# Hash attention with a mixture of adapters: signs made in place, adapter work regrouped, a tail with sums on TensorE

## The chip, the cores and the metric

The kernel runs on one core of a Trainium2 chip. The metric is device time in microseconds, from the first to the last instruction of the core. Three runs of the kernel before gave 201.65 us in the median (201.6 to 202.56). The engines are named as in the profile: PE is TensorE (matmul), PEld its weight loads, DVE is VectorE, ACT is ScalarE, POOL is GpSimd, SP is SyncE, which here only issues transfers.

## What is computed

Attention for 4 batches of 8 heads, 768 positions, 64 features. Each query and key is hashed to six sign bits by a projection, and a query attends only to keys with the same six bits. The result, seen as 3072 rows of 512 features, goes through a layer with eight low-rank adapters of which each row uses two.

```python
q_bits = (np.einsum('bhsd,dk->bhsk', q, proj) > 0)          # 6 bits
k_bits = (np.einsum('bhsd,dk->bhsk', k, proj) > 0)
mask = q_bucket[:, :, :, None] == k_bucket[:, :, None, :]
scores = np.where(mask, scale * q @ k.T, -1e9)
attn = softmax(scores)                                       # per query
x = (attn @ v).transpose(0, 2, 1, 3).reshape(3072, 512)
# adapters: E = 8, rank r = 16, the best two by gate
logits = x @ w_gate                                          # 3072 x 8
w = softmax over the two largest logits
out = x + sum over the two of  w * ((x @ A[e]) @ B[e])
```

## The kernel before

The work is cut into 16 **pairs** of heads (four per batch). One pair has nine **scores** steps, s = 0 to 8: TensorE fills a PSUM tile of 128 x 1024, ScalarE takes its exponential. Between the scores the program places the other work of the neighbouring pairs: transposes of q and k two pairs ahead, their hash one pair ahead, the weighted sum of the values, the norm. The hash becomes part of the score matmul: `aug` holds 64 rows of q or k, six sign rows (64 to 69) of plus or minus one half, and a constant row, so that scores of unequal buckets come out so low that their exponential vanishes.

```python
def score(self, p, s):
    ps = self.ps_s.tile([P, 1024], F32, tag="s")            # two buffers
    for h, kt, q, n, o in self.pieces(p, s):
        nc.tensor.matmul(out=ps[:, o:o + n], lhsT=aug[0:71, 2*h+1, kt*P:(kt+1)*P], rhs=q, ...)
    nc.scalar.activation(out=self.P_[p][:, s*1024:(s+1)*1024], in_=ps, func=ACT.Exp, scale=128.0)

def pair(self, p, s):                                        # after score(p, s)
    if s == 0: self.norm(p - 1, 0); self.trans(p + 1, 2)
    if s == 1: self.pvmm(p - 1, 1, 0, 2); self.cast(p + 1, 0); self.cast(p + 1, 1)
    if s == 2: self.hash(p + 1)
    if s == 3: self.uniform(p); self.pvmm(p - 1, 1, 2, 5)
    if s == 4: self.pvmm(p - 1, 1, 5, 6); self.norm(p - 1, 1); self.trans(p + 2, 0)
    if s == 5: self.vcast(p + 1); self.trans(p + 2, 1)
    if s == 6: self.pvmm(p, 0, 0, 2); self.xturn(p - 1); self.load(p + 3)
    if s == 7: self.pvmm(p, 0, 2, 4)
    if s == 8: self.pvmm(p, 0, 4, 6)
```

`trans` makes four fp32 transposes on TensorE into one of two `ps_t` buffers and a scaled copy (qkT) on VectorE; `cast` is a GpSimd copy of qkT to bf16 into aug; `hash` makes the signs of four heads and halves in four column tiles, one VectorE compare, and four small DMAs to move the signs to their rows. `pvmm` uses one `ps_v` buffer; `norm` reads it on VectorE and then lets GpSimd copy x to bf16 (xb), which a transposing DMA (`xturn`) turns into xT.

The adapters of batch b run during the pairs of batch b + 1, in groups of **slots** (a slot is 128 of the batch's 768 rows):

```python
def moe_slot(self, p, s):                                    # after pair(p, s)
    b, g = divmod(p - self.PPB - 1, self.PPB)                # PPB = 4 pairs a batch
    groups = ((0, 1), (2, 3), (4,), (5,)) if b < self.B - 2 else ((0, 1, 2), (3, 4, 5))
    ...
    if s == 1: self.lgz(b, slots); self.route_a(b, slots)
    if s == 2: self.route_b(b, slots)
    if s == 3: self.zmtrans(b, slots)
    if 0 <= s - 5 < len(slots): self.delta(b, slots, s - 5)

# lgz (PE):      lz = xT @ [w_gate | A]           one ps_m buffer, PSUM
# route_a (DVE): top = max8(lz gates); d = lz - top1; m = (lz >= top2); (ACT) e = exp(d)
# route_b (DVE): gw = m * e; zm = lz * gw; ss = sum(gw); rt = 1 / ss
# zmtrans (PE):  ztp = zm transposed; zmT = copy of ztp
# delta (PE):    dl = zmT @ Bcat;  (DVE) acc = dl * rt + x;  (SP) DMA of acc to the output
```

lz, ztp and dl share the one buffer of `ps_m`. Batch 3 has no pair after it. Its adapters run within the last pair and in the **tail** after the last exponential, in three groups of two slots; `third(u, part)` makes the weighted sum of the last pair for one third of the slots, `third_x` its normalised rows:

```python
def last_pair(self, p, b):                                   # t = the three groups
    ...
    if s == 3: self.xtrans(p - 1); self.third(0, 0)
    if s == 4: self.third(0, 1)
    if s == 5: self.xtrans(p, t[0]); self.third_x(0, x); self.lgz(b, t[0])
    if s == 6: self.route_a(b, t[0]); self.third(1, 0); self.route_b(b, t[0])
    if s == 7: self.third(1, 1); self.zmtrans(b, t[0], last=True)
    if s == 8: self.xtrans(p, t[1]); self.delta(b, t[0], 0, last=True); self.lgz(b, t[1]); ...
    # after the nine scores
    self.route_a(b, t[1]); self.third(2, 0); self.delta(b, t[0], 1, last=True)
    self.route_b(b, t[1]); self.zmtrans(b, t[1], last=True)
    self.third(2, 1)
    self.delta(b, t[1], 0, last=True)
    self.xtrans(p, t[2], on_act=True); self.lgz(b, t[2]); self.delta(b, t[1], 1, last=True)
    self.route_a(b, t[2]); ...; self.route_b(b, t[2]); self.zmtrans(b, t[2], last=True)
    for i in range(2): self.delta(b, t[2], i, last=True)
```

The **head** is the time before the first exponential. It loads the first pair head by head and makes the first head's signs:

```python
self.warm(19)                                                # small matmuls that keep TensorE busy
self.turn0(0)                                                # transposes and qkT copies, head 0
for e in range(2): nc.vector.tensor_copy(out=self.proj2[...], in_=self.pst[...])
self.half0(0, 0, nc.scalar.copy); self.warm(5)
self.hash0(0, (nc.gpsimd, nc.scalar))                        # hsf (PE), sgnf (DVE), two sign DMAs
self.half0(0, 1, nc.vector.tensor_copy)
self.turn0(1); self.half0(1, 0, nc.gpsimd.tensor_copy); self.half0(1, 1, nc.gpsimd.tensor_copy)
...
self.warm(12)
```

In pair 0 the second head's hash follows score 0 and the loads of pair 2 follow score 3; `load_moe` (the adapters' weights, six transfers issued by GpSimd) follows score 4.

Of the kernel before, what the change touches and what calls it, by code (L numbers as in the profile page):

```python
# [12 lines left out]
F32 = mybir.dt.float32  # L13
# [6 lines left out]
class Emitter:  # L20
# [45 lines left out]
    def prologue(self):  # L66
# [26 lines left out]
        self.warm(19)  # L93
        self.turn0(0)
        for e in range(2):
            nc.vector.tensor_copy(out=self.proj2[64 * e:64 * e + 64, e:12:2],
                                  in_=self.pst[64 * e:64 * e + 64, :])
        self.half0(0, 0, nc.scalar.copy)
        self.warm(5)
        self.hash0(0, (nc.gpsimd, nc.scalar))  # L100
        self.half0(0, 1, nc.vector.tensor_copy)
        self.turn0(1)
        self.half0(1, 0, nc.gpsimd.tensor_copy)
# [12 lines left out]
        self.Bcat = sg.tile([self.ER, self.Dm], BF16, name="Bcat")  # L116
        self.warm(12)


    def turn0(self, h):  # L120
        nc, P = self.nc, self.P
        for i in range(2):
            ps = self.ps_s.tile([P, 384], F32, tag="s", name=f"trf{h}_{i}")
            for u in range(3):
                nc.tensor.transpose(out=ps[:, u * P:(u + 1) * P],
                                    in_=self.nat[0][:, i, h, u * P:(u + 1) * P], identity=self.ident)
            out = self.qkT[0][:, (2 * h + i) * 384:(2 * h + i + 1) * 384]
            if i:
                nc.scalar.mul(out, ps, 2.0 ** -5)
            else:  # L130
                nc.vector.tensor_scalar(out=out, in0=ps, scalar1=2.0 ** -5, scalar2=None, op0=ALU.mult)

    def hash0(self, h, engs):
# [164 lines left out]
    def pvmm(self, p, h, i0, i1):  # L298
        if p < 0:
            return  # L300
        if i0 == 0:
            self.pv[p, h] = self.ps_v.tile([self.P, self.T, self.D + 1], F32, tag="v", name=f"pv{p}_{h}")
        for i in range(i0, i1):
            self.pv_mm(self.pv[p, h][:, i, :], p, h, i, True, True)
# [98 lines left out]
    def route_a(self, b, slots):  # L403
# [4 lines left out]
        for i in range(n):  # L408
# [3 lines left out]
                                op=ALU.subtract)  # L412
        m = self.smallp.tile([P, n, E], F32, tag="m", name=f"m{nm}")
        nc.vector.tensor_tensor(out=m, in0=lz[:, :, 0:E], in1=top[:, :, 1:2].to_broadcast([P, n, E]),
                                op=ALU.is_ge)
        e = self.smallp.tile([P, n, E], F32, tag="e", name=f"e{nm}")
        nc.scalar.activation(out=e, in_=d, func=ACT.Exp)  # L417
        self.me[b, slots] = m, e

    def route_b(self, b, slots):  # L420
        nc, P, E, r = self.nc, self.P, self.E, self.r
        lz, (m, e) = self.lz[b, slots], self.me[b, slots]
        n, nm = len(slots), f"{b}_{slots[0]}"
        zm = self.smallp.tile([P, n, self.ER], BF16, tag="zm", name=f"zm{nm}")
        rt = self.smallp.tile([P, n], F32, tag="rt", name=f"rt{nm}")
        gw = self.smallp.tile([P, n, E], F32, tag="gw", name=f"gw{nm}")
        nc.vector.tensor_mul(out=gw, in0=m, in1=e)  # L427
        nc.vector.tensor_tensor(  # L428
            out=zm.rearrange("p n (e r) -> p n e r", e=E),
            in0=lz[:, :, E:].rearrange("p n (e r) -> p n e r", e=E),  # L430
            in1=gw.unsqueeze(3).to_broadcast([P, n, E, r]), op=ALU.mult)
        ss = self.smallp.tile([P, n], F32, tag="ss", name=f"ss{nm}")
        nc.vector.tensor_reduce(out=ss, in_=gw, axis=AX.X, op=ALU.add)
        nc.vector.reciprocal(out=rt, in_=ss)
        self.zm[b, slots], self.rt[b, slots] = zm, rt

    def zmtrans(self, b, slots, last=False):
        nc, P = self.nc, self.P
        n = len(slots)
        ps = (self.ps_t if last else self.ps_m).tile(  # L440
            [P, n * P], BF16, tag="t" if last else "m", name=f"ztp{b}_{slots[0]}")
        for i in range(n):
# [8 lines left out]

    def delta(self, b, slots, i, last=False):
        nc, P, S = self.nc, self.P, self.S
# [3 lines left out]
        nc.tensor.matmul(out=ps, lhsT=self.zmT[b, slots][:, i * P:(i + 1) * P], rhs=self.Bcat,  # L457
                         start=True, stop=True)
        nc.vector.scalar_tensor_tensor(out=acc[:, i, :], in0=ps, scalar=self.rt[b, slots][:, i:i + 1],  # L459
                                       in1=self.x[b][:, slots[i], :], op0=ALU.mult, op1=ALU.add)  # L460
        rows = self.out[b * S:(b + 1) * S, :].rearrange("(p t) f -> p t f", t=self.T)
# [4 lines left out]


    def moe_slot(self, p, s):
        b, g = divmod(p - self.PPB - 1, self.PPB)
        if b < 0 or b > self.B - 2:  # L470
            return
        groups = ((0, 1), (2, 3), (4,), (5,)) if b < self.B - 2 else ((0, 1, 2), (3, 4, 5))
        if g >= len(groups):
            return
        slots = groups[g]
        if s == 1:
            self.lgz(b, slots)
            self.route_a(b, slots)
        if s == 2:
            self.route_b(b, slots)  # L480
        if s == 3:
            self.zmtrans(b, slots)
        if 0 <= s - 5 < len(slots):
            self.delta(b, slots, s - 5)

# [13 lines left out]
    def first_pair(self, s):  # L499
# [9 lines left out]
        if s == 4:  # L509
            self.hash(1)  # L510
            self.uniform(0)
            self.load_moe()
        if s == 5:
# [11 lines left out]
    def pair(self, p, s):  # L525
# [12 lines left out]
        if s == 4:  # L538
            self.pvmm(p - 1, 1, 5, 6)
            self.norm(p - 1, 1)  # L540
            self.trans(p + 2, 0)
        if s == 5:
            self.vcast(p + 1)
            self.trans(p + 2, 1)
        if s == 6:
            self.pvmm(p, 0, 0, 2)
# [7 lines left out]
    def last_pair(self, p, b):  # L554
        t = [(0, 1), (2, 3), (4, 5)]
        x = self.x[b][:, :, (self.PPB - 1) * self.P:]
        for s in range(9):
# [7 lines left out]
            if s == 3:  # L565
                self.xtrans(p - 1)
                self.third(0, 0)
            if s == 4:
                self.third(0, 1)
            if s == 5:  # L570
                self.xtrans(p, t[0])
                self.third_x(0, x)
                self.lgz(b, t[0])
            if s == 6:
                self.route_a(b, t[0])
                self.third(1, 0)
                self.route_b(b, t[0])
            if s == 7:
                self.third(1, 1)
                self.zmtrans(b, t[0], last=True)  # L580
            if s == 8:
                self.xtrans(p, t[1])
                self.delta(b, t[0], 0, last=True)
                self.lgz(b, t[1])
                self.third_x(1, x)
        self.route_a(b, t[1])
        self.third(2, 0)
        self.delta(b, t[0], 1, last=True)
        self.route_b(b, t[1])
        self.zmtrans(b, t[1], last=True)  # L590
        self.third(2, 1)
        self.delta(b, t[1], 0, last=True)
        self.xtrans(p, t[2], on_act=True)
        self.lgz(b, t[2])
        self.delta(b, t[1], 1, last=True)
        self.route_a(b, t[2])
        self.third_x(2, x)
        self.route_b(b, t[2])
        self.zmtrans(b, t[2], last=True)
        for i in range(2):  # L600
# [48 lines left out]
```

## Time and profile before

| what | us |
|---|---|
| median of three runs | 201.65 |
| head, to the first exponential | 11.18 |
| pair 0 | 14.56 |
| pairs 1 to 4 (no adapters), each | 8.92 to 9.44 |
| pairs 5 to 14 (adapters), together | 112.75 |
| pair 15, to the end of the last exponential | 13.77 |
| tail | 13.03 |

The stages are cut at the first exponential of each pair. Each line of the profile's tables names a line of the kernel, an engine and what it writes and reads (out<-in). A bracket behind a line of the timeline gives the idle time of the engine just before it and what ended that idle time. Matmuls are pipelined, so the busy time of PE overstates how full it is; the distance between the starts of neighbouring groups says more. The granted TensorE clock is given as a share of the full one.

### The profile page before, as it was taken

How to read it: one execution, taken by the hardware profiler on the slowest of the kernel's cores; microseconds unless marked ns; L12 is line 12 of the kernel's file. 1: busy time of each engine (PE TensorE's matmuls, PEld its weight loads, DVE VectorE, ACT ScalarE, POOL GpSimd, SP SyncE). 2: the span in 40 equal slices, each digit the busy share in tenths (PEclk: the TensorE clock that was granted, in tenths of full speed). 3: DMA queues.
4: the chain of work that ended last, by engine and by line, in shares of the span. 5: the costliest groups of instructions: out<-in, count | busy, mean ns of one | idle time of the engine just before them, and what ended most of it. 6: DMA issues, size and time to landing. Idle time of an engine off the chain costs nothing.

```text
span 201.6 us, 5215 instructions
## 1 busy us (share of the span) xinstructions
PE 168.3 (84%) x2072; PEld 116.0 (58%) x2078; DVE 128.4 (64%) x324; ACT 148.0 (73%) x166; POOL 111.0 (55%) x137
## 2 busy tenths in 40 slices
PE   7986699999999788789898798789898898779630
PEld 6653467676576665547575665557475564557410
DVE  4451356575565967777775867768775877634872
ACT  2367379999999777788887887779797677757420
POOL 8389966666867455655757353656566443610000
PEclk9999889999999999999999999999999999987995
DMA  5609972736559185490728294571818150610132
GB/s 173 221 3 298 194 119 50 236 68 220 104 184 226 61 198 188 84 300 28 243 75 255 77 229 159 141 243 59 274 60 264 37 181 6 141 59 3 72 137 104
DMA packets 32743, 29.11 MB, mean 144 GB/s; under 512 B 17494, under 2 KB 30672, under 8 KB 32720
## 3 DMA queue, kind: packets, MB, share of 16 engines
q1 hardware_dynamic: 27708, 28.50, 47.3%
q0 software_dynamic: 4864, 0.28, 4.2%
q8 instruction: 16, 0.26, 0.5%
q14 instruction: 7, 0.06, 0.1%
q10 hardware_dynamic: 148, 0.01, 0.1%
HBM read 19.42 MB, written 6.29 MB: 128 GB/s over the span
## 4 chain that ended last, share of the span: by engine, by line
PE 52%; DVE 19%; POOL 9%; issue 8%; DMA 7%; ACT 2%; SPq 1%; POOLq 0%; DVEq 0%
PE s L287 21%; PE pv L294 9%; PE tr L217 7%; PE hs L237 5%; DVE gw L427 4%; DMA nat<-in_k_dram 3%; DMA xT<-xb 3%; DVE acc L459 3%; DVE zm L428 3%; PE lz L399 3%; POOL vs L201 3%; DVE qkT L224 2%; POOL vb L199 2%; PE ztp L443 2%; POOL xb L335 2%
## 5 line engine op out<-in xcount | busy, mean ns | idle before, releaser
L289 ACT ACTIVATE P<-s 128x1024 bf16<-128x1024 f32 x144 | 141.9, 1023 | 32.3 <-PE s L287 29.6
L287 PE MATMUL s<-aug 71*128 71x256 bf16 (+1 forms) x396 | 88.0, 326 | 3.9 <-issue 1.0
L249 POOL CAST aug<-qkT 64x1536 bf16<-64x1536 f32 x30 | 43.8, 1460 | 21.8 <-DVE qkT L224 20.9
L294 PEld LDWEIGHTS <-P 128*128 128x128 bf16 x1080 | 43.5, 98 | 16.5 <-DVE x L329 6.4
L287 PEld LDWEIGHTS <-aug 71*128 71x128 bf16 x396 | 34.6, 99 | 30.4 <-issue 18.4
L294 PE MATMUL pv<-vb,P 128*128 128x65 bf16 x1080 | 47.9, 194 | 1.2 <-DVE x L329 1.2
L335 POOL CAST xb<-x 128x768 bf16<-128x768 f32 x15 | 12.3, 822 | 40.4 <-DVE x L329 34.0
L224 DVE TENSOR_SCALAR qkT<-tr 128x512 f32<-128x512 f32 x45 | 29.6, 682 | 5.7 <-PE tr L217 5.5
L324 DVE TENSOR_TENSOR pv<-pv,uni 128x390 f32<-128x390 f32 x30 | 17.2, 573 | 21.3 <-PE pv L294 21.2
L217 PE MATMUL tr<-ident,nat 128*128 128x128 f32 x180 | 28.2, 279 | 3.0 <-DMA nat<-in_k_dram 2.1
L217 PEld LDWEIGHTS tr<-ident,nat 128*128 128x128 f32 x180 | 21.2, 142 | 5.6 <-DMA nat<-in_k_dram 2.3
L459 DVE SCALAR_TENSOR_TENSOR acc<-dl,rt,x 128x512 f32<-128x512 f32 x24 | 17.8, 747 | 5.6 <-PE dl L457 4.5
L240 DVE TENSOR_SCALAR sgn<-hs 128x384 bf16<-128x384 f32 x15 | 8.4, 558 | 14.8 <-PE hs L237 14.8
L329 DVE TENSOR_TENSOR x<-pv,ri 128x384 f32<-128x384 f32 x30 | 16.7, 557 | 1.0
L201 POOL TENSOR_TENSOR vs<-vn 128x384 f32<-128x384 f32 x16 | 15.9, 991 | 0.0
L199 POOL CAST vb<-vn 128x768 bf16<-128x768 f32 x16 | 13.2, 825 | 0.1
L237 PE MATMUL hs<-qkT,proj 128*32 128x384 f32 x120 | 12.8, 498 | 0.0
L443 PE MATMUL ztp<-ident_bf,zm 128*128 128x128 bf16 x24 | 3.6, 225 | 10.7 <-DVE zm L428 10.6
L457 PE MATMUL dl<-Bcat,zmT 128*128 128x512 bf16 x18 | 6.8, 378 | 6.0 <-DVE acc L459 4.9
L399 PE MATMUL lz<-wa,xT 128*128 128x136 bf16 x96 | 8.8, 225 | 1.5 <-DMA xT<-xb 1.0
L427 DVE TENSOR_TENSOR gw<-m,e 128x16 f32<-128x16 f32 (+2 forms) x13 | 8.2, 633 | 1.1 <-ACT e L417 1.1
L443 PEld LDWEIGHTS <-zm 128*128 128x128 bf16 x24 | 1.5, 97 | 12.6 <-DVE zm L428 12.6
(61 smaller groups left out, 116.9 us busy)
## 6 DMA issues: line engine op xcount, KB each, us to landing
vn<-in_v_dram SPq DMA_DIRECT2D x16, 384.0 KB
nat<-in_q_dram SPq DMA_DIRECT2D x15, 384.0 KB
nat<-in_k_dram SPq DMA_DIRECT2D x15, 384.0 KB
out_dram<-acc SPq DMA_DIRECT2D x10, 256.0 KB
out_dram<-acc SPq DMA_DIRECT2D x4, 512.0 KB
out_dram<-acc SPq DMA_DIRECT2D x2, 768.0 KB
aug<-sgn SPq DMA_DIRECT2D x60, 9.0 KB
nat<-in_q_dram SPq DMA_DIRECT2D x2, 192.0 KB
```

Source lines behind the costliest of these rows:

```text
L199: nc.gpsimd.tensor_copy(out=vb[:, :, 0:T, 0:D], in_=vn)
L201: nc.gpsimd.tensor_add(out=s3, in0=vn[:, :, 0:3, :], in1=vn[:, :, 3:6, :])
L217: nc.tensor.transpose(out=ps[:, j * P:(j + 1) * P], in_=self.nat[p][:, idx % 2, idx // 2, u * P:(u + 1) * P], identity=self.ident)
L224: nc.vector.tensor_scalar(out=out, in0=ps, scalar1=2.0 ** -5, scalar2=None, op0=ALU.mult)
L237: nc.tensor.matmul(out=ps[32 * j:32 * j + 32, :], lhsT=self.proj2, rhs=self.qkT[p][:, j * 384:(j + 1) * 384], start=True, stop=True)
L249: self.nc.gpsimd.tensor_copy(out=self.aug[p % 2][0:64, :, e * n:(e + 1) * n], in_=self.qkT[p][64 * e:64 * e + 64, :].rearrange("p (j c) -> ...
L287: nc.tensor.matmul(out=ps[:, o:o + n], lhsT=aug[0:71, 2 * h + 1, kt * P:(kt + 1) * P], rhs=q, start=True, stop=True)
L289: nc.scalar.activation(out=self.P_[p][:, s * 1024:(s + 1) * 1024], in_=ps, func=ACT.Exp, scale=128.0)
L294: self.nc.tensor.matmul(out=pv, lhsT=self.p_at(p, h, kt, i), rhs=self.vb[p % 3][:, h, self.slot(kt), :], start=(start and kt == 0), stop=( ...
L324: nc.vector.tensor_tensor(out=pv[:, 0:T, :], in0=pv[:, 0:T, :], in1=self.uni[p][:, h:h + 1, :].to_broadcast([P, T, D + 1]), op=ALU.add)
L329: nc.vector.tensor_tensor(out=self.x[b][:, :, c:c + D].rearrange("p (u e) d -> p e u d", e=2), in0=pv[:, 0:T, 0:D].rearrange("p (e u) d -> ...
L459: nc.vector.scalar_tensor_tensor(out=acc[:, i, :], in0=ps, scalar=self.rt[b, slots][:, i:i + 1], in1=self.x[b][:, slots[i], :], op0=ALU.mu ...
```

## The change

It has five parts. (1) The first head's signs are computed by small matmuls whose output lands on the partitions of the sign rows, two row tiles of the array at a time, and VectorE writes them straight into aug; no DMA and no use of proj2, which is copied later. (2) The adapter groups of batches 0 and 1 become three pairs of slots. Routing no longer makes m: gw is made from lz, the second largest gate and e in one instruction per slot. The transposition moves from score 3 to 4, the deltas from 5 to 6. (3) In pairs with adapters, one of the qkT copies runs on ScalarE. (4) The adapters' weights are loaded in pair 2 instead of pair 0. (5) In the last pair, transposes and routing are placed later, one weighted sum uses another PSUM pool, and three outputs of the tail are summed on TensorE by an identity matmul of x in fp32 and copied out by ScalarE, one is added by VectorE from adapter rows already scaled. It is meant to take waits off the scores and the tail.

```diff
@@ prologue
-        self.turn0(0)
+        self.turn0(0, self.ps_s, "s")
+        self.half0(0, 0, nc.scalar.copy)
+        self.half0(0, 1, nc.scalar.copy)
+        self.signs0()
+        self.turn0(1, self.ps_t, "t")
         for e in range(2):
             nc.vector.tensor_copy(out=self.proj2[...], in_=self.pst[...])
-        self.half0(0, 0, nc.scalar.copy)
-        self.warm(5)
-        self.hash0(0, (nc.gpsimd, nc.scalar))
-        self.half0(0, 1, nc.vector.tensor_copy)
-        self.turn0(1)
...
-        self.warm(12)
+        self.warm(6)
+    def signs0(self):
+        for i in range(2):
+            hs = self.ps_s.tile([P, 2, 512], F32, tag="s", name=f"hsd{i}")
+            for e in range(2):
+                nc.tensor.matmul(out=hs[64:70, e, 0:384], lhsT=self.pst[64 * e:64 * e + 64, :],
+                                 rhs=self.qkT[0][64 * e:64 * e + 64, i * 384:(i + 1) * 384], ...)
+            nc.vector.tensor_scalar(out=self.aug[0][64:70, i, :]..., in0=hs[64:70, :, 0:384], ...)
@@ pvmm
+            pool, tag = (self.ps_t, "t") if (p, h) == (self.n_pairs - 2, 1) else (self.ps_v, "v")
@@ route_a, route_b
-        nc.vector.tensor_tensor(out=m, in0=lz[:, :, 0:E], in1=top[:, :, 1:2]..., op=ALU.is_ge)
-        nc.vector.tensor_mul(out=gw, in0=m, in1=e)
+        for i in range(n):
+            nc.vector.scalar_tensor_tensor(out=gw[:, i, :], in0=lz[:, i, 0:E], scalar=top[:, i, 1:2],
+                                           in1=e[:, i, :], op0=ALU.is_ge, op1=ALU.mult)
+        if last:                                   # tail: ss, rt, and gw scaled by rt
+            self.totals(b, slots, gw)
+            nc.vector.tensor_mul(out=gw, in0=gw, in1=self.rt[b, slots]...)
@@ delta
+        if by_pe:
+            nc.tensor.matmul(out=ps, lhsT=self.ident, rhs=self.x[b][:, slots[i], :], start=False, stop=True)
+            nc.scalar.copy(out=acc[:, i, :], in_=ps)
+        elif scaled:
+            nc.vector.tensor_add(out=acc[:, i, :], in0=ps, in1=self.x[b][:, slots[i], :])
@@ moe_slot
-        groups = ((0, 1), (2, 3), (4,), (5,)) if b < self.B - 2 else ((0, 1, 2), (3, 4, 5))
+        n = 2 if b < self.B - 2 else 3
+        slots = tuple(range(n * g, n * g + n))
-        if s == 3:
+        if s == 4:
             self.zmtrans(b, slots)
-        if 0 <= s - 5 < len(slots):
-            self.delta(b, slots, s - 5)
+        if 0 <= s - 6 < n:
+            self.delta(b, slots, s - 6)
@@ first_pair, pair
-            self.load_moe()                        # first_pair, s == 4
-            self.trans(p + 2, 0)
+            self.trans(p + 2, 0, on_act=self.has_moe(p))
+            if p == 2: self.load_moe()             # s == 5
@@ last_pair
-   s 3: xtrans(p - 1), third(0, 0)      s 5: xtrans(p, t0), third_x(0), lgz(t0)
-   s 6: route_a(t0), third(1, 0), route_b(t0)
-   s 7: third(1, 1), zmtrans(t0)        s 8: xtrans(p, t1), delta(t0, 0), lgz(t1), third_x(1)
-   then: route_a(t1), third(2, 0), delta(t0, 1), route_b(t1), zmtrans(t1), third(2, 1),
-         delta(t1, 0), xtrans(p, t2), lgz(t2), delta(t1, 1), ...
+   s 3: third(0, 0)                     s 5: xtrans(p - 1), xtrans(p, t0), third_x(0)
+   s 6: lgz(t0), route_a(t0), third(1, 0)
+   s 7: third(1, 1), route_b(t0, last)  s 8: xtrans(p, t1), third_x(1), zmtrans(t0), lgz(t1)
+   then: third(2, 0), route_a(t1), delta(t0, 0, by_pe), route_b(t1, last), third(2, 1),
+         delta(t0, 1, by_pe), zmtrans(t1), xtrans(p, t2), lgz(t2), delta(t1, 0, scaled),
+         route_a(t2), third_x(2), route_b(t2), delta(t1, 1, by_pe), zmtrans(t2), ...
```

The last hunk is written out as lists of calls; the code of the other hunks is cut where it only names tiles.

## The prediction

> **What bounds the kernel now.** I read the page's first table, then ScalarE's timeline, to cut the span into pieces, then the busy time by piece, and only then the waits inside a piece. The page:
>
> ```profile
> PE 168.3 (84%) x2072; PEld 116.0 (58%) x2078; DVE 128.4 (64%) x324; ACT 148.0 (73%) x166; POOL 111.0 (55%) x137
> ```
>
> No engine is full over the whole span. ScalarE runs 144 exponentials (16 head pairs of 9); cut at the first one of each pair, the busy time by stage reads as follows (us from:to, length, busy us and count of each engine, granted clock, DMA):
>
> ```profile
> 11.18:25.74 14.56, 10.91 (x95) 6.86 (x95) 5.56 (x11) 8.89 (x10) 13.49 (x21) 0.92 1.03 182
> ...
> 53.10:62.05 8.95, 8.79 (x119) 6.15 (x118) 5.29 (x12) 8.66 (x10) 6.39 (x7) 1.00 0.64 160
> 62.05:73.90 11.85, 9.98 (x131) 6.94 (x130) 8.75 (x23) 9.13 (x11) 6.84 (x8) 1.00 0.53 153
> ...
> 85.75:96.15 10.40, 9.30 (x124) 6.46 (x124) 7.92 (x21) 8.91 (x11) 6.07 (x7) 1.00 0.51 170
> ...
> 151.10:163.60 12.50, 10.87 (x139) 7.52 (x138) 9.07 (x25) 9.25 (x12) 6.72 (x8) 1.00 0.48 133
> 163.60:174.80 11.20, 9.78 (x126) 5.86 (x124) 8.37 (x22) 8.83 (x12) 6.36 (x7) 1.00 0.34 91
> 174.80:188.57 13.77, 10.74 (x146) 8.38 (x148) 6.36 (x22) 9.41 (x12) 0.84 (x2) 0.88 0.16 59
> 188.57:201.60 13.03, 3.72 (x46) 2.03 (x44) 7.46 (x26) 1.55 (x6) 0.00 (x0) 0.84 0.33 121
> ```
>
> A pair without adapters takes 8.95 us and is **ScalarE bound**: nine exponentials, about 0.977 us from start to start, are 8.79. A pair with an adapter group of two slots takes 11.85, of one slot 10.40, of three 12.50 and 11.20, though ScalarE's work hardly grows. The ten pairs 5 to 14 last 174.8 - 62.05 = 112.75 us; at 8.95 each they would be 89.5, so the adapters cost 23 us in the middle. Head (to 11.18), pair 0 (14.56), the last pair (13.77) and the tail (13.03) are the other losses. ScalarE in pair 5:
>
> ```profile
> 64.30 0.21 ACT L417 ACTIVATE e<-d 128x16 f32<-128x16 f32 x1 [0.24 <-DVE d L411]
> 64.42 2.17 ACT L289 ACTIVATE P<-s 128x1024 bf16<-128x1024 f32 x2
> 67.64 3.20 ACT L289 ACTIVATE P<-s 128x1024 bf16<-128x1024 f32 x3 [1.05 <-PE s L287]
> 71.98 3.91 ACT L289 ACTIVATE P<-s 128x1024 bf16<-128x1024 f32 x4 [1.13 <-PE s L287]
> ```
>
> Two stalls of 1.05 and 1.13 us for scores that TensorE brings late, and 0.24 before the small exponential. The other engines, same time:
>
> ```profile
> 63.37 2.98 POOL L249 CAST aug<-qkT 64x1536 bf16<-64x1536 f32 x2 [0.80 <-DVE qkT L224]
> 65.53 0.84 DVE L427 TENSOR_TENSOR gw<-m,e 128x16 f32<-128x16 f32 x1
> 66.89 0.28 PE L443 MATMUL ztp<-ident_bf,zm 128*128 128x128 bf16 x2 [0.75 <-DVE zm L428]
> 69.14 1.28 DVE L224 TENSOR_SCALAR qkT<-tr 128x512 f32<-128x512 f32 x2
> 71.13 0.38 PE L457 MATMUL dl<-Bcat,zmT 128*128 128x512 bf16 x1 [0.98 <-DVE acc L459]
> ```
>
> TensorE works in order. It stands 0.75 us at ztp for VectorE's gw and zm, and 0.98 us at the second dl, whose only buffer is freed by the first acc, queued behind two qkT copies. Each stand appears at ScalarE as one of the two stalls.
>
> **What the skill says.** (1) The Trainium skill, SBUF — State Buffer, "Who interferes with whom": a VectorE instruction with two SBUF inputs is blocked by a GpSimd instruction that reads SBUF; with one such input it is not. The trace agrees: gw multiplies two SBUF tiles and ends at 66.37, where the GpSimd cast ends (63.37 + 2.98 = 66.35); in the tail, where GpSimd is idle, the same form takes 0.16 to 0.17 us. (2) TensorEngine Tiling (Array Packing), "Key Properties": different tiles of the array run in parallel. That is what the new first signs rest on; here only the column form is seen: one four-head hash, four matmuls into four column tiles, takes 0.78 us on the chain. (3) DMA: Bandwidth & Descriptors, "Issuing engines are not separate DMA queues": all transfers share 16 engines and interleave. The trace fits: the weights' software queue has 4864 packets and 4.2% of 16 engines' span (8.5 us on every engine), issued from 17.97 on, while k of pair 2 is under way. (4) TensorE: Matmul & The Clock Gate, "What's actually happening": TensorE runs at half clock until some microseconds of steady work. The trace agrees: the warming matmuls still take 0.116 us per 128 columns at 8.5 to 9.9 (0.91 ns a column), the scores of the steady state 0.43 us per 1024 (0.42 ns).
>
> **The change, part by part.**
>
> *Adapter pairs.* Groups become three of two slots in batches 0 and 1 (pairs 5, 6, 7 and 9, 10, 11) and two of three in batch 2 (13, 14); pairs 8 and 12 have none. gw now reads lz in PSUM and one SBUF tile, so it doesn't wait for GpSimd: 0.84 (1.06 for one slot) becomes two instructions of about 0.17; the m instruction (0.16) goes. ztp moves one score later, when zm is long done: the stall of 1.05 goes. The deltas move to scores 6 and 7, and one qkT copy (0.64) leaves VectorE just ahead of them: the 1.13 goes. New on ScalarE: that copy. Its 384-column form takes 0.49 us, the 1024-column exponential 1.02, so 512 columns are an estimated 0.60, 0.55 with overlap.
>
> ScalarE's sum for a two-slot pair: 8.95 + small exponential 0.13 + wait before it 0.2 + copy 0.55 = 9.8. TensorE's: scores 9 x 0.43, 72 weighted sums at 0.030 = 2.2, three groups of transposes 1.3, hash 0.8, uniform 0.1 = 8.25; adapters lz 0.47, ztp 0.11, dl 0.43 = 1.0; 9.25 together. Against ScalarE's slot of 0.98 per score it is over by 0.2 to 0.3 in each of scores 1, 2 and 4, and there is 0.4 of slack (the second score buffer lets TensorE start 0.98 early, and a tile needs 0.58 from its first matmul to its exponential), so some 0.15 of stall stays: **9.95**. VectorE has about 8.1. The three-slot pairs: lz 0.70, a longer wait for the exponential, three acc of 0.75 ahead of the next norm: 10.3 for pair 13, 10.2 for pair 14 (no copy, as no pair follows to transpose). Sum 6 x 9.95 + 2 x 8.95 + 20.5 = 98.1 against 112.75: **-14.6**. I take off 0.6 for order effects I can't see: -14.0.
>
> *Head.* Before:
>
> ```profile
> 5.75 1.50 PE L138 MATMUL hsf<-qkT,proj 128*32 128x384 f32 x4
> 7.32 0.55 DVE L141 TENSOR_SCALAR sgnf<-hsf 64x384 bf16<-64x384 f32 x1 [1.62 <-PE hsf L138]
> 7.91 0.86 ACTq L151 DMA_DIRECT2D aug<-sgnf  x1
> 10.55 0.59 PE L287 MATMUL s<-aug 71*128 71x512 bf16 x3 [0.65 <-DMA aug<-sgnf]
> ...
> 21.79 0.33 PE L217 MATMUL tr<-ident,nat 128*128 128x128 f32 x1 [2.11 <-DMA nat<-in_k_dram]
> ```
>
> The signs' DMA, from 7.91 to 10.55, goes: they are written in place. In return TensorE makes q's and k's signs one after the other, an estimated 1.3 us each at the slow clock (the same columns took up to 1.50 above, two tiles side by side, and 0.84 later at the full clock): 5.2 to 7.8; VectorE's k sign (768 elements on six partitions, estimated 0.95) ends near 8.8; the second head's transposes and six warm matmuls put the first score at about 9.4 instead of 10.55. The second head's hash waits for proj2, now copied later, which gives back part: **-0.9** by the time pair 0 runs.
>
> *Pair 0.* Without the weights' packets, and with the queue freed earlier, k of pair 2 should land about 1.5 us sooner: **-1.5**. The weights now load in pair 2, where GpSimd has about 2.5 us idle per pair for 4.9 us of issuing and where loads have 7 us of lead; **+0.3** for a collision in pair 3.
>
> *Last pair and tail.* ScalarE waits 4.4 us for scores in the last pair: 1.08 behind TensorE's wait for the one pv buffer (now another pool), 2.28 behind its wait for GpSimd's xb (the transposes move from score 3 to 5). Both go; with some new waits for signs of routing, 13.77 becomes about 10.7: **-3.0**. After the last exponential, third(2,1) no longer stands behind ztp of the middle group (TensorE waits 1.39 there), but two outputs get an fp32 identity matmul of 512 columns, an estimated 1.04 us each (0.78 x 512/384) and more at a granted clock of 0.84, ahead of the last transposes: near a draw, **-0.2**.
>
> Sum: 201.65 - 14.0 - 0.9 - 1.5 + 0.3 - 3.0 - 0.2 = 182.35; I say 183, as unforeseen waits only add.
>
> **Rivals.** *TensorE becomes the bound.* Its busy time is near the length of a plain pair (8.79 of 8.95), which speaks for it; the issue sum of 8.25 speaks against. If it were full, a two-slot pair would be 8.95 + 1.0 plus some waits, 10.3 or more, and the total 185 to 186. *The copy on ScalarE costs what the wait gave*: true if the second dl would have found its buffer free through the spacing alone; then 0.55 x 7 = 3.9 us are wasted, though the total above already pays for it. *The weights collide*: with 8.5 us of packets per engine beside pair 5's loads, q and k could come after their transposes; +1 to +2. *Row tiles do not overlap*: the first signs take twice as long, the head loses 1.5 instead of gaining 0.9. *The identity matmuls sit on the last chain*: +1.5 in the tail. Any two of these leave 186 to 187; only all with a stall left in each adapter pair reach 190.
>
> **Range and chances.** 179.5 to 188. The stalls removed are seen in the trace one by one, and a 2% gain is 4 us, a quarter of the sum: faster 0.96, within 2% 0.03, slower 0.01.
>
> **What would show it.** Right: gw near 0.17 us while GpSimd casts; no wait of ztp for zm nor of dl for acc in the middle; two-slot pairs 9.8 to 10.2, pairs 8 and 12 at 8.95; first exponential near 10; no 2.1 us wait for k in pair 0; the last pair under 11. Wrong: two-slot pairs above 10.5 with ScalarE still waiting for scores; a new wait of tr for its load in pair 3; the first score later than 10.5; the last exponential to the end over 14.

## The result and the profile after

Four runs of the changed kernel gave 185.91 us in the median (184.52 to 187.59), four of the kernel before 202.11 (201.6 to 204.01): a ratio of 0.916, with a 95% interval of 0.907 to 0.925. Executions of one kernel differed by 1 to 8 us, and the ratios leave disturbed ones out while the medians do not, so what follows rests on stages and waits of the profiles first. The profiled execution of the changed kernel has a span of 185.8 us, that of before 201.6.

The row of the exponentials in the list of costly groups, changed kernel (busy us, mean ns, then ScalarE's idle time ahead of them and its main releaser):

```profile
L301 ACT ACTIVATE P<-s 128x1024 bf16<-128x1024 f32 x144 | 140.2, 1026 | 12.8 <-PE s L299 10.9
```

and the same row of the kernel before:

```profile
L289 ACT ACTIVATE P<-s 128x1024 bf16<-128x1024 f32 x144 | 141.9, 1023 | 32.3 <-PE s L287 29.6
```

ScalarE's wait for scores fell from 29.6 to 10.9 us, by 18.7; the span fell by 15.8. The busy time by stage, changed kernel (from:to, length, busy of PE, PEld, DVE, ACT and POOL, granted clock, DMA share, GB/s): pair 0, pair 3, a two-slot pair, the three-slot pair 14, the last pair and the tail.

```profile
9.04:23.40 14.36, 11.24 (x95) 7.13 (x96) 5.68 (x12) 8.89 (x9) 10.37 (x19) 0.90 0.56 189
...
41.56:51.44 9.88, 9.09 (x120) 6.22 (x119) 5.92 (x13) 8.71 (x10) 9.70 (x11) 1.00 1.73 160
71.10:81.10 10.00, 9.83 (x132) 6.84 (x131) 7.68 (x22) 9.28 (x13) 6.40 (x8) 1.00 0.79 196
...
150.95:162.21 11.26, 9.93 (x137) 6.31 (x135) 8.04 (x24) 9.00 (x10) 6.38 (x7) 1.00 0.33 93
162.21:171.39 9.18, 8.03 (x134) 6.67 (x129) 6.39 (x23) 8.76 (x10) 0.82 (x1) 1.00 0.22 88
171.39:185.80 14.41, 6.91 (x60) 3.82 (x61) 7.27 (x28) 2.72 (x7) 0.00 (x0) 0.95 0.30 110
```

The two-slot pair is down from 11.85 to 10.00 and the last pair from 13.77 to 9.18, though each has about ScalarE's work of before. Pair 0 has hardly moved, pair 3 is longer by 0.9, and the tail by 1.4. In the timeline of a two-slot pair (the chain through routing, ScalarE's copy, and the second delta):

```profile
62.54 2.98 POOL L261 CAST aug<-qkT 64x1536 bf16<-64x1536 f32 x2 [1.69 <-DVE qkT L236]
64.73 0.35 DVE L437 SCALAR_TENSOR_TENSOR gw<-lz,top,e 128x8 f32<-128x8 f32 x2
66.26 0.28 PE L463 MATMUL ztp<-ident_bf,zm 128*128 128x128 bf16 x2
66.73 0.59 ACT L234 ACTIVATE qkT<-tr 128x512 f32<-128x512 f32 x1
67.20 5.77 ACT L301 ACTIVATE P<-s 128x1024 bf16<-128x1024 f32 x6
69.27 0.38 PE L477 MATMUL dl<-Bcat,zmT 128*128 128x512 bf16 x1
```

No bracket stands behind ztp or dl: TensorE no longer waits for zm or for a free buffer. gw takes 0.35 us for two slots in the middle of the GpSimd cast (62.54 to 65.52) instead of 0.84, and after the copy six exponentials follow without a wait.

### The profile page after: what moved, and what is told of

Read it like the earlier page. It is cut to its first block, busy times and chain, and to the rows that moved or that the text cites. A ratio compares the mean times of both kernels' runs of the same rounds, so it can differ in the third digit from the quotient of the medians.

```text
span 185.8 us, 5197 instructions
## 1 busy us (share of the span) xinstructions
PE 167.4 (90%) x2076; PEld 114.2 (61%) x2077; DVE 118.2 (64%) x306; ACT 151.2 (81%) x173; POOL 110.3 (59%) x136
## 4 chain that ended last, share of the span: by engine, by line
PE 60%; DVE 15%; DMA 12%; SPq 4%; issue 3%; POOL 2%; ACT 1%; DVEq 0%; ACTq 0%; POOLq 0%
PE s L299 22%; PE pv L306 14%; DMA nat<-in_k_dram 12%; PE tr L229 6%; PE hs L249 5%; PE dl L477 3%; DVE pv L337 3%; DVE x L342 3%; PE lz L412 3%; SPq L388 2%; DVE acc L485 2%; POOL xb L348 1%; DVE ri L340 1%; PE pvl L370 1%; PE warm L180 1%
## 5 line engine op out<-in xcount | busy, mean ns | idle before, releaser
L301 ACT ACTIVATE P<-s 128x1024 bf16<-128x1024 f32 x144 | 140.2, 1026 | 12.8 <-PE s L299 10.9
L299 PE MATMUL s<-aug 71*128 71x256 bf16 (+1 forms) x396 | 87.0, 323 | 2.6 <-issue 1.1
L299 PEld LDWEIGHTS <-aug 71*128 71x128 bf16 x396 | 34.4, 98 | 24.2 <-issue 10.9
L229 PE MATMUL tr<-ident,nat 128*128 128x128 f32 x180 | 29.2, 280 | 3.7 <-DMA nat<-in_k_dram 2.8
L236 DVE TENSOR_SCALAR qkT<-tr 128x512 f32<-128x512 f32 x38 | 25.6, 685 | 6.8 <-PE tr L229 5.9
L485 DVE SCALAR_TENSOR_TENSOR acc<-dl,rt,x 128x512 f32<-128x512 f32 x20 | 14.9, 751 | 8.0 <-PE dl L477 8.0
L213 POOL TENSOR_TENSOR vs<-vn 128x384 f32<-128x384 f32 x16 | 15.9, 992 | 0.0
L427 ACT ACTIVATE e<-d 128x16 f32<-128x16 f32 (+1 forms) x11 | 2.4, 217 | 8.8 <-DVE d L424 8.7
L477 PE MATMUL dl<-Bcat,zmT 128*128 128x512 bf16 x23 | 8.4, 378 | 0.8 <-ACT zmT L467 0.5
L412 PE MATMUL lz<-wa,xT 128*128 128x136 bf16 x96 | 7.9, 223 | 1.0 <-ACT xT L402 0.6
L216 POOL TENSOR_TENSOR vb<-vs,vs 128x128 bf16<-128x128 f32 x16 | 7.3, 458 | 1.3
L215 POOL TENSOR_TENSOR vs<-vs 128x128 f32<-128x128 f32 x16 | 7.3, 454 | 1.3
```

The costliest lines, as they stand in the source:

```text
L213: nc.gpsimd.tensor_add(out=s3, in0=vn[:, :, 0:3, :], in1=vn[:, :, 3:6, :])
L229: nc.tensor.transpose(out=ps[:, j * P:(j + 1) * P], in_=self.nat[p][:, idx % 2, idx // 2, u * P:(u + 1) * P], identity=self.ident)
L299: nc.tensor.matmul(out=ps[:, o:o + n], lhsT=aug[0:71, 2 * h + 1, kt * P:(kt + 1) * P], rhs=q, start=True, stop=True)
L301: nc.scalar.activation(out=self.P_[p][:, s * 1024:(s + 1) * 1024], in_=ps, func=ACT.Exp, scale=128.0)
```

## The experiments

All are edits of the changed kernel, but for the head alone. A length of a pair is the distance between first exponentials (the windows above are cut to within 0.1 us of them), the tail runs from the end of the last exponential to the end of the span. Each ratio is to the kernel before, run beside it.

**Three parts of the adapter pair, undone one at a time.** First the spacing:

```diff
-        if s == 4:
+        if s == 3:
             self.zmtrans(b, slots)
-        if 0 <= s - 6 < n:
-            self.delta(b, slots, s - 6)
+        if 0 <= s - 5 < n:
+            self.delta(b, slots, s - 5)
```

> The changed kernel with the adapters' transposition back at score 3 and the deltas back at score 5. Theory: the block of gw and the queue of copies made most of the two stalls, and both are gone by other means; ztp then waits 0.2 to 0.4 us for zm, dl little for acc, the two-slot pairs grow to 10.2 to 10.6 us and the total by 1.5 to 4 us. Rival: the spacing is what removed the stalls; then the two-slot pairs go back to 11 us or more and the total grows by 8 us or more.

193.67 us (ratio 0.958, 0.948 to 0.967). The six two-slot pairs took 10.86, 10.87, 10.87, 11.34, 10.86 and 11.23 us instead of 9.75 to 10.54: together 66.0 instead of 60.2, between what theory and rival said. The list of waits in pair 5 names both old waits again (total, times, longest):

```profile
ACT P L301 <- PE s L299: 1.1, 2, 0.6
...
PE dl L477 <- DVE acc L485: 0.5, 1, 0.5
...
PE ztp L463 <- DVE zm L442: 0.3, 1, 0.3
```

So the spacing alone is worth about 0.97 us a pair, the largest single part.

Then the qkT copy, back on VectorE:

```diff
-            self.trans(p + 2, 0, on_act=self.has_moe(p))
+            self.trans(p + 2, 0, on_act=False)
```

> The changed kernel with the qkT copy of the adapter pairs left on VectorE. Theory of the prediction: the copy had to leave, because it stands ahead of acc; without the move the second dl waits for acc again and the two-slot pairs stay at 10.0 us or grow to 10.5; total 0 to +3 us. Rival: the later deltas alone free the buffer in time, and the copy only adds 0.55 us to a full ScalarE; then the two-slot pairs fall to 9.5 us and the total by 2.5 to 4 us.

187.98 us (0.925, 0.913 to 0.936). Pairs 6 and 7 took 10.20 each instead of 9.98; all six 61.4 instead of 60.2. Its total can't be told from that of the changed kernel, but the lengths of these two pairs repeat to a few hundredths in five other profiles with that copy on ScalarE (9.98 to 10.00). ScalarE's 0.59 us therefore returns about 0.2 net.

Then the old gate, with m and a multiplication of two SBUF tiles:

```diff
-        for i in range(n):
-            nc.vector.scalar_tensor_tensor(out=gw[:, i, :], in0=lz[:, i, 0:E], scalar=top[:, i, 1:2],
-                                           in1=e[:, i, :], op0=ALU.is_ge, op1=ALU.mult)
+        nc.vector.tensor_mul(out=gw, in0=m, in1=e)          # m made in route_a, as before
```

> The changed kernel with the routing of before: a mask m, and gw as the product of two SBUF tiles. Theory: with the transposition one score later the block by GpSimd is hidden. Then gw takes 0.8 to 1.0 us again while GpSimd casts, ztp still waits for nothing, and the total is within 0.7 us of the changed kernel's. Rival: VectorE's delay passes on to the norm, to the one buffer of the weighted sums and to the copies. Then each adapter pair grows by 0.3 to 0.5 us and the total by 2.5 to 4 us.

187.66 us (0.924, 0.912 to 0.936). Pairs 6 and 7 took 10.23 each, all six 61.6: about 0.25 a pair. gw takes 0.84 us again in the median and ztp waits for nothing in pair 5: with the wider spacing, most of what the wait for GpSimd cost is already hidden. The three parts undone singly make 1.4 us of the 1.86 by which pair 6 fell (11.84 to 9.98); the rest belongs to no one of them, and no run undoes two at once.

**Four groups instead of three**, the rest of the change kept:

```diff
-        n = 2 if b < self.B - 2 else 3
+        groups = ((0, 1), (2, 3), (4,), (5,)) if b < self.B - 2 else ((0, 1, 2), (3, 4, 5))
+        slots = groups[g]
+        n = len(slots)                      # has_moe too: the copy on ScalarE in all four
```

> The changed kernel with the old groups of slots (two pairs of slots and two single ones in batches 0 and 1), all else new. Theory: the regrouping itself is worth little within the pairs (two single-slot pairs at 9.6 to 9.8 us each against 10.0 and 9.1), but the free fourth pair lets the transposing transfer land before the next batch's first adapter pair; without it that pair waits 0.5 to 2 us for xT again, and the total grows by 1.5 to 4 us. Rival: the fourth pair is where a quarter of the gain comes from: single-slot pairs stay near 10.4 us and the total grows by 3 us without any wait for xT.

184.95 us (0.918, 0.912 to 0.923). The two pairs with one slot, 7 and 8, took 9.72 and 9.46, together 19.18, against 9.98 + 9.17 = 19.15 for one pair with two slots and one with none. Regrouping is a draw: pairs 5 to 12 are 78.1 us here and 78.6 there, and TensorE waits for no xT in pair 9, so neither theory nor rival was right.

**The weights back in pair 0.**

```diff
@@ first_pair, s == 4
             self.uniform(0)
+            self.load_moe()
@@ pair, s == 5
-            if p == 2:
-                self.load_moe()
```

> The changed kernel with one part undone: the adapters' weights load in pair 0 again. Theory: their packets collide with the loads and sign transfers of pairs 3 and 4 and had little to do with pair 0's wait. Then pairs 3 and 4 fall from 9.9 us to about 8.95 each, pair 0 grows by less than 0.7 from 14.4, and the total is 1 to 2 us below the changed kernel's (about 184.5). Rival: the move freed pair 0 by as much as it costs later. Then pair 0 grows by 1.5 us or more and the total is equal or higher.

186.01 us (0.917, 0.908 to 0.926): the same total, with an interval of 1.8 us to either side, about as wide as what was to be seen. Pairs 3 and 4 went back from 9.81 and 9.85 to 8.96 each, but pair 0 took 14.48, as with the weights elsewhere. So the weights cost 1.7 us where the change put them, and in pair 0 nothing that stands out from that pair's spread (12.1 to 15.7 in seven profiles with this pair 0 and the weights in pair 2). How they cost it, in pair 3 of the changed kernel's timeline:

```profile
42.92 3.52 POOL L171 DMA_DIRECT2D wa<-in_moe_A_dram  x4
46.95 3.04 POOL L261 CAST aug<-qkT 64x1536 bf16<-64x1536 f32 x2
50.75 0.59 PE L299 MATMUL s<-aug 71*128 71x512 bf16 x3 [0.77 <-DMA aug<-sgn]
```

GpSimd issues six transfers from 42.01 to 47.0, and its cast starts only then. The first score of pair 4 waits 0.77 us, by the profile for the signs' DMA, which came after the end of the cast (49.99); the DMA share of this stage, 1.73, is the highest of those shown above. From the cast the chain of waits goes on into pair 4:

```profile
48.53 1.47 POOL aug L261
...
50.90 1.24 SPq L388
...
52.82 3.83 DMA nat<-in_k_dram
56.69 0.33 PE tr L229
```

xb stands behind the cast, the transposing DMA behind xb, and the next loads behind that one in SyncE's queue: they are issued at 52.19, with the weights in pair 0 at 48.99 (where pair 3 starts 0.6 us earlier). What this profile saved, its tail lost: 15.95 us instead of 14.42, at a granted clock of 0.61 in its first 4 us.

**What bounds pair 0.** If the weights don't, the loads' queue may: the second head's signs are two DMAs on SyncE (issued from 10.82 to 12.61), and k of pair 2 is issued behind them, at 13.65. Here the loads go ahead:

```diff
         if s == 0:
-            self.hash0(1, (self.nc.sync, self.nc.sync))
             self.load_v(1)
+            self.load(2)                         # and no longer at s == 3
+            self.hash0(1, (self.nc.sync, self.nc.sync))
```

> The changed kernel with the loads of pair 2 (and v of pair 1) issued ahead of the second head's sign transfers, for which the issuing queue stands waiting until 10.8 us. Theory: pair 0's wait for the keys of pair 2 (1.5 us, and 0.7 for the queries) is a late issue and not the weights; it goes, and pair 0 falls from 14.4 to 12 us or less, the total by 2 us or more. Rival: the small sign transfers now land behind 1.6 MB of loads; score 4 waits for them, and pair 0 stays at 13.5 us or more.

185.54 us (0.904, 0.896 to 0.912). TensorE's waits from 8 to 30 us, changed kernel:

```profile
PE tr L229 <- DMA nat<-in_k_dram: 1.5, 1, 1.5
PE tr L229 <- DMA nat<-in_q_dram: 0.7, 1, 0.7
```

and with the loads early:

```profile
PE s L299 <- DMA aug<-sgnf: 1.1, 1, 1.1
```

The wait for keys is gone, and the signs' DMA, now behind the loads, takes its place; pair 0 is 12.92 us. The queue was the cause, but one transfer was exchanged for another. So the second head's signs were made in place as well, and no DMA is left:

```diff
+    def signs1(self, i):                     # i = 0: q, 1: k; two row tiles, one bank each
+        for e in range(2):
+            pool, tag = ((self.ps_m, "m"), (self.ps_v, "v"))[e]
+            hs = pool.tile([P, 384], F32, tag=tag, ...)
+            nc.tensor.matmul(out=hs[64:70, :], lhsT=self.pst[64 * e:64 * e + 64, :], rhs=self.qkT[0]...)
+            nc.vector.tensor_scalar(out=self.aug[0][64:70, 2 + i, ...], in0=hs[64:70, :], ...)
@@ first_pair
-            self.hash0(1, (self.nc.sync, self.nc.sync))
+        if s < 2:
+            self.signs1(s)
```

> The changed kernel with the second head's signs also made in place, by the same small matmuls into the two idle PSUM buffers, so that pair 0 has no sign transfer, and with the loads of pair 2 issued at about 4 us. Theory: pair 0 loses about 2 us to waiting and then 2 us more because TensorE, idle for over a microsecond, is granted half its clock afterwards; without the wait the clock stays at 1.0 and pair 0 takes 11 to 12.3 us instead of 13 to 15.7; total 2 us or more under the changed kernel. Rival: the clock drops at 18 to 24 us in any case (a start-up matter); pair 0 stays at 13 us or more without a wait for keys.

183.65 us (0.912, 0.905 to 0.919, which can't be told from the changed kernel's 0.916). Pair 0 took 10.86 us, 3.5 less, TensorE is busy for 10.62 of them and waits for no transfer, and the clock of the stage is 1.00, where the changed kernel has 0.90. In the changed kernel it falls after the waits (0.63, then 0.52 from 22 to 24 us):

```profile
18.00:20.00 2.00, 0.78 (x10) 0.53 (x10) 0.24 (x1) 0.00 (x0) 1.80 (x3) 1.00 0.36 111
20.00:22.00 2.00, 2.00 (x26) 1.54 (x23) 1.14 (x2) 1.14 (x2) 0.00 (x0) 0.63 0.92 315
```

TensorE is busy 0.78 of 2 us, and then runs 4 us at little over half the clock.

**The head alone**, put into the kernel before (its diff is the prologue hunk of the change: signs0, turn0 with a pool, proj2 later, warm 6).

> The kernel before with only the new head: the first signs in place, proj2 copied later, fewer warming matmuls. Theory: the first exponential comes at 8 to 9 us instead of 11.2 and pair 0 keeps its length of 14.5, so the total falls by 2 to 3 us. Rival: what is won in the head is lost in pair 0, which waits for the keys of pair 2 in any case; then pair 0 grows by 1.5 us or more and the total falls by less than 1 us.

204.36 us against 203.47 for the kernel before beside it: 1.0005, 0.996 to 1.005. In the profile the head is 2.7 us and pair 0 1.8 us shorter, and pairs 9 and 13 give most of that back: 13.16 instead of 11.95 and 14.92 instead of 12.33. TensorE's longest wait in pair 9:

```profile
PE lz L410 <- DMA xT<-xb: 1.8, 1, 1.8
```

On the chain of waits this transposing DMA took 4.27 us, against 3.06 in the kernel before, where lz waits 0.6; pair 13 has the same wait of 1.8, and after it a clock of 0.52 for 3 us. The gain ahead may have moved this DMA against the loads that share its engines; that the loads delayed it is inferred from their times, not tested.

**The tail without identity matmuls**: the three outputs are added by VectorE.

```diff
-        self.delta(b, t[0], 0, last=True, by_pe=True)       # and two more
+        self.delta(b, t[0], 0, last=True, scaled=True)
```

> The changed kernel without the identity matmuls: the three outputs that TensorE summed and ScalarE copied are added by VectorE (0.69 us each), as the scaled one is. Theory of the prediction: near a draw, within 0.5 us. Rival 1: two identity matmuls of 1.0 to 1.4 us stand ahead of the last weighted sum and the last transposes; without them the tail is 1 to 2 us shorter. Rival 2: VectorE's additions stand ahead of the routing; the tail is 0.7 to 1.5 us longer.

186.28 us (0.916, 0.906 to 0.925): no difference to be seen. In its profile the tail was 16.33 us at a clock of 0.50 to 0.66 in its first 4 us, so its work at full clock was not seen. Two kernels with the identity matmuls whose clock fell 0.5 to 0.9 us after the last exponential, as here (weights in pair 0, copy on VectorE), had tails of 15.95 and 15.96; but without them the clock fell a second time, from 7.5 us after the last exponential on.

**The changed kernel again**, beside these runs:

> The changed kernel itself, unaltered, on the chip of the runs below, as their yardstick: its first profile shows pairs 3 and 4 at 9.9 us and a tail of 14.4 us at the full TensorE clock, while the profile with the weights back in pair 0 shows these pairs at 8.95 but the same median. Theory: the collision is in every execution; pairs 3 and 4 read 9.5 to 10.2 us each again. Rival: it was a chance of that execution; one or both read 9.0. For the tail: 14.4 us if the granted clock stays at 1.0, 15.5 to 16 if it drops to 0.6 to 0.7 for some microseconds as in the other profiles.

187.65 us (184.67 to 189.88). Pairs 3 and 4 took 9.10 and 10.77: the theory's size in sum, split otherwise. In all nine profiles with the weights in pair 2 the two pairs are 19.5 to 19.9 us together, with the weights elsewhere 17.9 to 18.0. Pairs 5 to 14 repeat those of the first profile to 0.1 us, but for pairs 8 (9.53 against 9.17) and 9 (10.69 against 10.54); pair 0 was 15.68, the tail 14.59 at a clock of 1.00 in its first 12 us.

**Towards a better version.** To the kernel with both heads' signs in place the weights were added in three parts, in pairs 1, 2 and 3:

```diff
-            if p == 2:
-                self.load_moe()
+            if 1 <= p <= 3:
+                self.load_moe(p - 1)         # gate and A[0] | A[1], A[2] | A[3] and B
```

> The run before it (second head's signs in place, early loads) with the weights' six transfers spread over pairs 1, 2 and 3, two each. Theory: the collision in pairs 3 and 4 came from 4.5 us of GpSimd issuing and 4832 packets at once; a third of it fits in GpSimd's idle time; pairs 1 to 4 read 8.95 to 9.3 us each, 1.5 to 2 us less together than with all in pair 2. Rival: any packet of the weights delays a sign transfer; pairs 2 to 4 grow by 0.3 to 0.7 us each and nothing is won.

183.64 us (0.903, 0.894 to 0.912), no better in the median than without (183.65). Pairs 3 and 4 fell to 8.96 each, from 9.11 and 10.68, and pairs 5 and 6 rose from 9.72 and 9.98 to 10.96 and 11.11 (in the next kernel, with the same spread, to 9.73 and 10.89), with new waits at TensorE in these two pairs:

```profile
58.37 0.47 PE L426 MATMUL lz<-wa,xT 128*128 128x136 bf16 x5 [1.06 <-DMA xT<-xb]
...
73.07 0.33 PE L243 MATMUL tr<-ident,nat 128*128 128x128 f32 x1 [0.91 <-DMA nat<-in_k_dram]
```

Last, the three-slot pairs' deltas one score earlier with one more acc buffer, and the last third's weighted sum ahead of the identity matmuls:

```diff
-        if 0 <= s - 6 < n:
-            self.delta(b, slots, s - 6)
+        if 0 <= s - (6 if n == 2 else 5) < n:
+            self.delta(b, slots, s - (6 if n == 2 else 5))
@@ tail
+        self.third(2, 1)
         self.delta(b, t[0], 0, last=True, by_pe=True)
         self.route_b(b, t[1], last=True)
-        self.third(2, 1)
```

> The run before it with two more changes, told apart by stage. In the three-slot pairs the deltas start one score earlier. In the tail the last weighted sum stands ahead of the identity matmuls, the middle group is added by VectorE, and the output tile has three buffers. Theory: pair 14 waits less for its small exponential (1.5 us before) and the two three-slot pairs fall from 22.4 us to 21 or less together; third(2,1) starts within 2.2 us of the last exponential instead of 3.2 and the tail at full clock is 13.0 to 13.6 us instead of 14.4. Rival for the tail: the chain from the last routing on is unchanged and the drop of the granted clock eats the rest; tail 14.4 us or more.

182.42 us (0.904, 0.898 to 0.911), the lowest median of all, though its interval overlaps those of the two kernels before it. In the three-slot pairs its edit gained nothing: they took 11.13 and 11.30, because new waits (1.3 us of dl for zmT in pair 14) replaced the old one. The tail was 14.59 us, with a clock of 0.50 from 2.1 to 5.5 us after the last exponential. The kernel with early loads has the changed kernel's tail, and its clock fell for the same stretch; its tail took 16.15. The step before the fall and the fall itself, in the early loads and in the last kernel (last exponential ended at 169.37 and 166.24):

```profile
168.08:171.49 3.41, 1.63 (x29) 1.32 (x30) 2.52 (x13) 1.29 (x2) 0.00 (x0) 1.00 0.00 0
171.49:174.91 3.42, 3.42 (x19) 1.94 (x16) 1.93 (x9) 0.80 (x2) 0.00 (x0) 0.50 0.00 0
```

```profile
164.88:168.29 3.41, 1.62 (x28) 1.24 (x28) 2.52 (x13) 1.36 (x2) 0.00 (x0) 1.00 0.00 0
168.29:171.71 3.42, 3.42 (x27) 2.08 (x23) 1.99 (x10) 0.68 (x2) 0.00 (x0) 0.50 0.00 0
```

At like clock the new order of the tail is thus 1.6 us shorter, in one profile of each.

## Why the prediction was right, and where its steps were not

The predicted 183 us against 185.91 lies within the range. By its own steps, from the two profiles:

| step | predicted | measured |
|---|---|---|
| pairs 5 to 14 | -14.0 | -11.7 |
| head | -0.9 | -2.1 |
| pair 0 | -1.5 | -0.2 |
| collision of the weights | +0.3 | +1.7 |
| last pair | -3.0 | -4.6 |
| tail | -0.2 | +1.4 |
| pairs 1 and 2 | 0 | -0.2 |

The steps miss by +6.6 us and by -3.0, so that part of the total's agreement is luck.

*Adapter pairs: the mechanism right, one term mis-sized.* Two-slot pairs were put at 9.95 and took 9.75 to 9.98 (pair 9: 10.54); pairs 8 and 12 were put at 8.95 and took 9.17 each. The largest miss is that of the three-slot pairs, put at 10.3 and 10.2, which took 11.11 and 11.26. Pair 13 took 10.35 to 10.38, as predicted, in four other profiles with the same adapter code; here, as in pair 9, a transpose stands 0.4 us for a load of k. The mis-sized term is that of pair 14: 11.25 to 11.30 in all nine profiles with its code, and 11.26 between first exponentials in the kernel before, so it did not fall at all. In pair 14:

```profile
152.56 0.54 PE L306 MATMUL pv<-vb,P 128*128 128x65 bf16 x12 [0.84 <-DVE x L342]
...
154.42 0.22 ACT L427 ACTIVATE e<-d 128x24 f32<-128x24 f32 x1 [1.53 <-DVE d L424]
```

The working named the longer wait for the exponential and the three acc ahead of the norm, but gave both together 1.3 us over a plain pair: ScalarE alone waits 1.53 for d, and TensorE 0.84 for x. *The copy on ScalarE costs what the wait gave* fell: undone, the pairs are longer by 0.2. *TensorE becomes the bound* is not seen in the two-slot pairs, where six exponentials run without a wait; its total of 185 to 186 came true by other terms.

*Head: right in kind, too small.* q's and k's sign matmuls together took 2.40 us from 4.90 (2.6 estimated, from 5.2), the last sign was ready at 8.31 and the first score began at 8.41, not 9.4. *Row tiles do not overlap* fell with that. But alone, this part is worth nothing.

*Pair 0: the step that was wrong.* I held the weights' packets for a cause of the late keys; without them TensorE waited 0.7 for q and 1.5 for k of pair 2, and with them 0.8 and 1.2. The loads' place in SyncE's queue is the cause, and the fall of the clock behind the waits is a term I did not have.

*The weights: a rival came true*, at the upper end of its +1 to +2, though not by full DMA engines alone: on the chain stands GpSimd, whose 5 us of issuing hold up the cast, xb and, through SyncE's queue, the next loads. I had counted 2.5 us of idle GpSimd per pair for 4.9 us of issuing and still put the cost at 0.3.

*Last pair and tail*: -4.6 and +1.4 where -3.0 and "near a draw" were said; together -3.2, as predicted. The border between them moved: work that stood ahead of the last exponential now stands behind it. ztp and lz wait there for the routing of the first group, and the first part of the last weighted sum starts 1.65 us after the last exponential (171.39), in the kernel before 0.12 (its line comes last):

```profile
171.73 0.28 PE L463 MATMUL ztp<-ident_bf,zm 128*128 128x128 bf16 x2 [1.05 <-DVE zm L442]
172.45 0.63 PE L412 MATMUL lz<-wa,xT 128*128 128x136 bf16 x8 [0.44 <-DVE zmT L469]
173.04 0.65 PE L370 MATMUL pvl<-vb,P 128*128 128x65 bf16 x16
...
188.69 0.65 PE L357 MATMUL pvl<-vb,P 128*128 128x65 bf16 x16
```

From there the chain of waits passes through two identity matmuls (1.02 us each, 1.04 estimated), the first of which stands ahead of the last part of that sum:

```profile
173.74 1.02 PE L480 MATMUL dl<-x,ident 128*128 128x512 f32 x2
174.60 0.41 PE L370 MATMUL pvl<-vb,P 128*128 128x65 bf16 x8
```

That part starts 3.2 us after the last exponential, in the kernel before 2.5. Taking the identity matmuls out showed no shorter tail; moving this part, and the last group's transposes and gates, ahead of finished outputs (and one of these to VectorE) gave 1.6 us at like clock. So the order is worth about what the tail lost; how the 1.4 us divide between the moved border and the identity matmuls is argued, not shown. Two of the prediction's own signs of being wrong came: the tail over 14 us, and the wait of tr for its load behind the weights (0.4 us, in pair 4 and not 3). Not run: weights in pair 0 together with both heads' signs in place.

## What to carry to other kernels

Where engines work in order, the distance between a producer and its consumer in program order can be worth more than a faster producer: here one score of spacing gave 0.97 us a pair, the faster gate and the moved copy 0.2 to 0.25 each. A transfer that comes late is traced back to the queue in which it was issued before bandwidth is blamed. And each part of a change is read where it ends: a head and pair 0 shorter by 4.5 us were worth nothing once TensorE waited for a DMA further on.

## What the runs showed of the hardware

Waits of TensorE of about a microsecond can be followed by a fall of its clock. In pair 0 TensorE waited one to three times for transfers, 0.4 to 1.8 us each, in ten profiles of kernels with the new head; in eight of them the granted clock then fell, to 0.50 (pair 0 of 12.9 to 15.7 us). In the ninth and tenth it stayed at 1.00 (12.12 and 12.78), though the waits of the ninth, 0.8 and 0.4 us, are nearly those of one of the eight, 0.9 and 0.4. Without waits, with both heads' signs in place, there was no fall. The Trainium skill, TensorE: Matmul & The Clock Gate, "What's actually happening", gives an idle window of about 3.4 us for the fall, one that runs free of the program. No single wait here is as long, so a wait well below that length is not safe. The traces agree with a free-running step: in all fourteen profiles each change of the granted clock comes a whole number of 3.41 us after the one before (changed kernel: 20.50, 23.91 and 184.34 us, 1 and 47 steps apart), and where the steps lie differs between executions of one kernel. In pair 0 it is how much of one step the waits take that separates the profiles: in the step before the fall TensorE was busy for 0.96 to 2.13 of 3.41 us in the eight, in the least busy step of the other two for 2.14 and 2.19, too near to read a limit from. The changed kernel, with a fall, then the tail without identity matmuls, with none:

```profile
17.09:20.50 3.41, 1.80 (x21) 1.34 (x22) 0.69 (x1) 1.00 (x2) 2.68 (x4) 1.00 0.59 189
20.50:23.91 3.41, 3.41 (x25) 2.61 (x24) 1.99 (x4) 2.08 (x3) 0.00 (x0) 0.50 0.95 324
```

```profile
14.94:18.35 3.41, 2.19 (x31) 1.52 (x29) 0.56 (x3) 2.00 (x3) 3.27 (x4) 1.00 0.91 327
18.35:21.76 3.41, 3.26 (x50) 2.43 (x46) 2.82 (x6) 3.16 (x4) 0.88 (x2) 1.00 0.71 230
```

In the tail the same work met either clock. From 6 us before the end of the last exponential to 2 us after it, the changed kernel and that with the weights in pair 0 show the same busy times of TensorE (1.98, 2.00, 0.99 and 1.22 of each 2 us). In the 4 us after the end the clock is 1.00 in the one and 0.72, then 0.50 in the other; the tails are 14.42 and 15.95 us. The steps tell them apart. In six profiles one began 0.7 to 1.0 us before the end of the last exponential, and the clock stayed at 1.00 for 12 us and more (tails of 14.2 to 14.9 us). In the six others one began 1.3 to 2.9 us before it, and at its end the clock fell (15.9 to 16.3 us, and 14.59 in the last kernel). The changed kernel, then the tail without identity matmuls:

```profile
170.69:174.10 3.41, 1.88 (x28) 1.60 (x30) 2.27 (x12) 0.91 (x2) 0.00 (x0) 1.00 0.00 0
174.10:177.51 3.41, 2.86 (x26) 1.61 (x25) 1.86 (x8) 1.45 (x3) 0.00 (x0) 1.00 0.21 77
```

```profile
165.13:168.54 3.41, 2.04 (x32) 1.40 (x29) 2.38 (x12) 2.35 (x4) 0.00 (x0) 1.00 0.03 5
168.54:171.95 3.41, 2.99 (x35) 2.58 (x34) 1.15 (x6) 0.22 (x1) 0.00 (x0) 0.50 0.00 0
```

No run moves the steps on purpose, and the busy time of a step does not decide alone: 1.88 of 3.41 us kept the clock in the one, 2.04 did not in the other. What else counts stays open.
